# Attention's output kept with features on partitions: one product on GpSimd in place of turns on TensorE

## The chip, the cores and the metric

The kernel runs on one core of a Trainium2 chip. Its five engines work side by side, each through its own list of instructions in order: TensorE (PE) multiplies matrices into PSUM, VectorE (DVE) and ScalarE (ACT) work elementwise and can read PSUM, GpSimd (POOL) works elementwise on SBUF alone, and SyncE (SP) does nothing here but issue transfers. ScalarE issues some transfers too. The metric is the device time of one launch in microseconds; lower is better.

## The reference

One input x of 2048 rows and 640 features goes through two branches, and a gate mixes them per row:

```python
g = _sigmoid((x * gate_w).sum(-1, keepdims=True))
a = _A_ref(x, A_wq, A_wk, A_wv, A_wo, A_beta)
b = _B_ref(x, B_w1, B_w3, B_w2)
return g * a + (1 - g) * b
```

Branch b is a gated FFN of width 1728: `(silu(x @ w1) * (x @ w3)) @ w2`. Branch a is attention with 32 heads of 20 features over 4 segments of 512 rows, plus a memory that is carried from segment to segment:

```python
logits = jnp.einsum("bhqd,bhkd->bhqk", qs, ks) * scale + mask
p = _softmax(logits, axis=-1)
a_dot = jnp.einsum("bhqk,bhkd->bhqd", p, vs)
pq = phi(qs)
num = jnp.einsum("bhld,bhde->bhle", pq, M)
den = jnp.einsum("bhld,bhd->bhl", pq, z)[..., None] + 1e-6
a_mem = num / den
o = g * a_mem + (1.0 - g) * a_dot
...
M = M + jnp.einsum("bhld,bhle->bhde", pk, vs)
z = z + jnp.einsum("bhld->bhd", pk)
```

Here `phi(t)` is t + 1 above zero and exp(t) below, g is a sigmoid of one number per head, and the mask adds -1e9 where the key's row lies before the query's, so a query sees itself and later keys. The heads' outputs, side by side, are multiplied by `wo`.

## The kernel before

**Precision.** Dense products run as three passes over operands split into a rounded part and a rest (`split`, L91: ScalarE copies the rounded part, GpSimd or VectorE subtracts). Queries and keys are split in three bfloat16 parts (`split3`).

**Dense work.** The segments c = 0 to 3 are handled in two pairs, A = (0, 1) and B = (2, 3). For each pair the program projects v, k and q, builds the memory (`memory_turn`, `memory_write`), and runs the FFN in five groups of hidden blocks (`ffn_up`, `ffn_down`) and the output projection (`oproj`). Each of these is a generator that yields an estimate in ns after every piece of work.

**Attention.** `attention` (L598) walks one head at a time over 4 x 32 heads, in ten steps per head: the scores and their row maxima (`s_unit`), then, three heads later, the transposed scores with the maxima taken off through three extra rows of the query operand (`st_unit`), exp on ScalarE, zeroing of the triangle on GpSimd (L551), and for every four heads the product with v (`pv_quad`, L556). v carries a column of ones, so that the product also holds the softmax sums. In `pv_quad` the four heads stand at partitions 0, 32, 64 and 96: 20 features, the sum, and 11 unused rows. ScalarE copies the result to `oq` (L565).

**The step of the output.** One head later `o_quad` (L570) turns `oq` with four TensorE transposes (L581) into PSUM, so that rows of x lie on partitions. VectorE takes reciprocals of the sums (L584), multiplies by 1 - g (L585) and scales (L589, L592). Where there is a memory (c > 0), GpSimd adds the result to memory's part (L593), which has been loaded into the ring `oring` (L578). `oproj` needs features on partitions again: `turn` transposes the ring's blocks (L646 to L652), and each is split from PSUM (L92, L93).

**Memory's read.** `memory_read` (L258) makes, for four row blocks and two halves of the heads, the products of phi(q) with the memory (L272), then four VectorE instructions (L277 to L280): add 1e-6, reciprocal, times g, scale. The result `gm` goes to DRAM (`gd`) by SyncE and comes back by L578.

**What sets the order.** The main loop at the end lays dense pieces between attention's steps: a segment's dense estimates are spread evenly over its steps as a credit. `braid(a, b, n)` puts one piece of b after every n pieces of a and the rest of b behind a; `weave(a, b, n)` puts all of b behind piece n of a. TensorE's list stands as the source has it. The lists of the other four engines, SyncE's included, are put in order by a planner that simulates the program.

**Transfers by counted steps.** `store_later` puts a store off by four steps. Weights go through `w_load` (a transfer into one of `NRAW` = 2 raw buffers), `w_split` (four steps later, into one of `NW` = 6 tiles) and `w_get`, which forces both where they have not happened. `load_pair` (L472) loads queries and keys of two heads (`qst`, `kst`) into one of three places; `max_rows` (L522) sends the maxima's rows into `qst` (L526).

Of the kernel before, what the change touches and what calls it, by code (L numbers as in the profile page):

```python
# [26 lines left out]
NST, NW, NRAW, NHT, NVG, ND = 3, 6, 2, 6, 2, 3  # L27
KR = 6 * DH
LAG_T, LAG_P, NP, AGE = 3, 4, 4, 4
# [5 lines left out]
def gated_mix(ctx: ExitStack, tc: tile.TileContext, xT, wqk, wv, w13, w2, w2h, wo, beta, out):  # L35
# [10 lines left out]
    gd = [dp.tile([P, 4, D], F32, name=f"gd{c}") for c in range(NSEG)]  # L46
# [3 lines left out]
    mask = cp.tile([P, L], F32, name="mask")  # L50
# [3 lines left out]
    cH = cp.tile([P, H], F32, name="cH")  # L54
    nsT = [cp.tile([P, 32], BF, name=f"ns{i}") for i in range(2)]
    oring = cp.tile([P, 4, 960], F32, name="oring")
# [4 lines left out]
    def constants():  # L61
# [10 lines left out]
        nc.scalar.activation(gH, gH, AF.Exp, scale=-1.0)  # L72
        nc.vector.tensor_scalar(gH, gH, 1.0, None, op0=ALU.add)
        nc.vector.reciprocal(gH, gH)
        nc.vector.tensor_scalar(cH, gH, -1.0, 1.0, op0=ALU.mult, op1=ALU.add)
# [40 lines left out]
    raws, clock = [], dict(step=0, oldest=0, next=0)  # L116
# [141 lines left out]
    def memory_read(c):  # L258
        pq = big.pop(("q", c))[:, :KB * L].rearrange("p (b n) -> p b n", b=KB)
        for qb in range(4):  # L260
            gm = ht_tile([P, D], F32, f"gm{c}_{qb}")
            for hf in range(2):
                ps = dense_bank(f"nd{c}_{qb}_{hf}")
                nd = ps[:, :16 * VE].rearrange("p (h e) -> p h e", e=VE)
                todo = []
                for b in range(KB):
                    a0, a1 = HEADS[b]
                    u0, u1 = max(a0, 16 * hf), min(a1, 16 * hf + 15)
                    if u0 <= u1:
                        todo.append((b, a0, u0, u1))  # L270
                for n, (b, a0, u0, u1) in enumerate(todo):
                    nc.tensor.matmul(nd[:, u0 - 16 * hf:u1 - 16 * hf + 1, :],  # L272
                                     pq[:, b, qb * P:(qb + 1) * P],
                                     Ms[c - 1, b][:, u0 - a0:u1 - a0 + 1, :],
                                     start=n == 0, stop=n == len(todo) - 1, skip_group_check=True)
                r = sp.tile([P, 16], F32, tag="r16", name="nd_r")
                nc.vector.tensor_scalar(r, nd[:, :, DH], 1e-6, None, op0=ALU.add)  # L277
                nc.vector.reciprocal(r, r)
                nc.vector.tensor_mul(r, r, gH[:, 16 * hf:16 * hf + 16])
                nc.vector.tensor_mul(  # L280
                    gm[:, 320 * hf:320 * hf + 320].rearrange("p (h e) -> p h e", e=DH),
                    nd[:, :, :DH], r.unsqueeze(2).broadcast_to([P, 16, DH]))
                yield 700
            store_later(gd[c][:, qb, :], gm, ("g", c, qb))

    def v_blocks(c, iv):
# [7 lines left out]
        for lb in range(4):  # L294
# [5 lines left out]
            for hf in range(2):  # L300
# [77 lines left out]
    def job_read(c):  # L378
        return 5.6, memory_read(c)

    def job_v(cs):
        iv = [w_add(wv[i], D + 2) for i in range(KB)]
        return [(17.8, v_blocks(c, iv)) for c in cs]
# [86 lines left out]
    oall, heads = {}, {}  # L470

# [50 lines left out]
    def max_rows(j):  # L522
# [3 lines left out]
        nc.sync.dma_start(heads[j]["pair"][KR:KR + 3].rearrange("a h (b n) -> a (h b) n", n=P), mr[:24])  # L526
# [29 lines left out]
    def pv_quad(j):  # L556
# [9 lines left out]
        bank["ot"] = ot  # L566
# [3 lines left out]
    def o_quad(j):  # L570
        c, h = heads[j]["c"], heads[j]["h"]
        g, hl = h // 16, h % 16
        if hl == 0:
            at = 320 * ((2 * c + g) % 3)
            oall[c, g] = oring[:, :, at:at + 320]
            if c:
                assert ("g", c, 3) in stored
                nc.sync.dma_start(oall[c, g], gd[c][:, :, 320 * g:320 * g + 320])  # L578
        pt = pp.tile([P, L], F32, tag="o", name=f"oc{j}", bufs=1)
        for qb in range(4):  # L580
            nc.tensor.transpose(pt[:, qb * P:(qb + 1) * P], bank["ot"][:, qb * P:(qb + 1) * P], ident)  # L581
        o = pt.rearrange("p (b h e) -> p b h e", b=4, e=32)
        rc = sp.tile([P, 4, 4], F32, tag="rc", name="rc")
        nc.vector.reciprocal(rc, o[:, :, :, DH])  # L584
        nc.vector.tensor_mul(rc, rc, cH[:, h:h + 4].unsqueeze(1).broadcast_to([P, 4, 4]))  # L585
        rb = rc.unsqueeze(3).broadcast_to([P, 4, 4, DH])
        dst = oall[c, g][:, :, DH * hl:DH * hl + 4 * DH].rearrange("p b (h e) -> p b h e", e=DH)
        if c == 0:
# [273 lines left out]
```

## Time and profile before

| | us |
|---|---|
| median of 3 runs | 1186.91 |
| lowest, highest | 1186.42, 1190.69 |
| the profiled execution's own time | 1187.66 |
| its span | 1185.9 |

The profile shows one execution: busy time of each engine, windows by stage, groups of equal instructions with their mean length and the idle time before them with what ended it, waits, the chain of work that ended last, and the timeline. L12 is line 12 of the kernel before. PEld is TensorE's loading of weights, beside its matmuls. SPq and ACTq are the queues from which SyncE and ScalarE issue transfers. The granted TensorE clock is 1.0 over the whole span.

### The profile page before, as it was taken

The numbers are of one execution on the slowest core, as the hardware profiler recorded it, in microseconds if no ns is written. First come the engines' busy times: TensorE is split into PE (matmuls) and PEld (weight loads), VectorE is DVE, ScalarE is ACT, GpSimd is POOL, SyncE is SP. The second block draws the span as 40 slices with busy tenths as digits, with TensorE's granted clock in tenths as the row PEclk, the third lists the DMA queues.
The fourth block names the chain that finished last, engine by engine and source line by source line (L and its number), as shares of the span: only waits on it lengthen the run. The fifth ranks groups of instructions, "written<-read, shape, count | busy, mean of one in ns | idle before, by whom it ended". The sixth has DMA issues, their size and how long they took to land.

```text
span 1185.9 us, 20067 instructions
## 1 busy us (share of the span) xinstructions
PE 1157.3 (98%) x7093; PEld 884.9 (75%) x7093; DVE 674.0 (57%) x2186; ACT 493.3 (42%) x955; POOL 470.7 (40%) x591
## 2 busy tenths in 40 slices
PE   8989999999999999999999999999999999999998
PEld 5977766767767887877967667677767776776997
DVE  6034566456755553566245787756676676663434
ACT  6255434444244233153355554435543344334131
POOL 6065434154144234245065543334343344335232
PEclk9999999999999999999999999999999999999999
DMA  8474632232233143315257674263323243321012
GB/s 287 149 221 167 231 95 69 73 100 69 57 90 90 57 140 85 101 51 170 99 184 241 191 240 141 79 179 84 97 68 96 73 119 79 85 68 46 23 56 89
DMA packets 99460, 137.58 MB, mean 116 GB/s; under 512 B 9120, under 2 KB 69024, under 8 KB 99360
## 3 DMA queue, kind: packets, MB, share of 16 engines
q1 hardware_dynamic: 83616, 117.69, 33.4%
q10 hardware_dynamic: 15744, 18.62, 4.5%
q8 instruction: 56, 0.92, 0.3%
q14 instruction: 44, 0.36, 0.1%
HBM read 89.75 MB, written 46.14 MB: 115 GB/s over the span
## 4 chain that ended last, share of the span: by engine, by line
PE 79%; DVE 7%; issue 6%; DMA 3%; ACT 2%; POOL 2%; SPq 0%; DVEq 0%; ACTq 0%; POOLq 0%
PE g L206 16%; PE u L206 15%; PE f L458 13%; PE o L562 6%; PE s L499 6%; PE op L665 5%; PE q L206 4%; PE t L537 4%; PE v L306 3%; PE k L206 2%; POOL W L93 2%; PE nd L272 1%; PE pm L361 1%; DVE junk L506 1%; PE oc L581 1%
## 5 line engine op out<-in xcount | busy, mean ns | idle before, releaser
L506 DVE CUSTOM_DVE_ANT_0 junk<-s,mask 128x128 bf16<-128x128 f32 (+3 forms) x512 | 249.7, 488 | 204.2 <-PE s L499 195.0
L545 ACT ACTIVATE P<-t 128x384 f32<-128x384 f32 (+1 forms) x384 | 201.8, 527 | 331.7 <-PE t L542 118.6
L93 POOL TENSOR_TENSOR W<-wr,W 128x640 fp32r<-128x640 f32 (+1 forms) x126 | 196.9, 1567 | 166.9 <-ACT W L92 152.6
L551 POOL TENSOR_SCALAR_AFFINE_SELECT P<-P 128x256 f32<-128x256 f32 x256 | 105.0, 411 | 351.0 <-ACT P L545 338.4
L206 PE MATMUL g<-X,W 128*128 128x512 f32 x840 | 242.2, 423 | 0.0
L206 PE MATMUL u<-X,W 128*128 128x512 f32 x780 | 227.1, 426 | 0.0
L458 PE MATMUL f<-W,ht 128*128 128x320 f32 x1312 | 224.6, 321 | 1.9 <-DVE acc L463 1.9
L458 PEld LDWEIGHTS f<-W,ht 128*128 128x128 f32 x1312 | 199.2, 189 | 8.3 <-DVE acc L463 2.6
L206 PEld LDWEIGHTS g<-X,W 128*128 128x128 f32 x840 | 152.4, 190 | 25.9 <-issue 1.9
L206 PEld LDWEIGHTS u<-X,W 128*128 128x128 f32 x780 | 141.7, 191 | 22.1 <-issue 1.2
L499 PE MATMUL s<-kst,qst 120*128 120x128 bf16 (+3 forms) x512 | 135.4, 305 | 4.2 <-DVE m L506 2.3
L92 ACT CAST W<-wr 128x640 fp32r<-128x640 f32 (+1 forms) x133 | 95.4, 724 | 61.8 <-DMA wr<-in_w_dram 22.1
L463 DVE SCALAR_TENSOR_TENSOR acc<-f,cgate,acc 128x320 f32<-128x320 f32 x128 | 70.1, 550 | 59.6 <-PE f L458 59.0
L93 POOL TENSOR_TENSOR ht<-ft,ht 128x512 fp32r<-128x512 f32 x52 | 67.4, 1296 | 81.4 <-ACT ht L92 80.9
L537 PE MATMUL t<-qst,kst 123*128 123x512 bf16 (+1 forms) x256 | 93.1, 364 | 1.0 <-ACT P L545 1.0
L665 PE MATMUL op<-W,oT 128*128 128x320 f32 x480 | 87.7, 326 | 1.3 <-POOL W L93 0.6
L499 PEld LDWEIGHTS <-qst 120*128 120x128 bf16 x512 | 44.4, 99 | 56.2 <-issue 46.9
L206 PE MATMUL q<-X,W 128*128 128x512 f32 x300 | 81.6, 415 | 3.0 <-POOL X L93 1.1
L206 PE MATMUL k<-X,W 128*128 128x512 f32 x300 | 80.3, 412 | 2.0 <-DVE ks_t L239 2.0
L306 PE MATMUL v<-W,X 128*128 128x320 f32 (+1 forms) x480 | 76.6, 317 | 1.8 <-ACT W L92 0.8
L665 PEld LDWEIGHTS op<-W,oT 128*128 128x128 f32 x480 | 73.2, 190 | 3.9 <-POOL W L93 1.5
L562 PE MATMUL o<-P,vg 128*32 128x512 f32 (+3 forms) x1024 | 75.5, 436 | 0.0
(106 smaller groups left out, 1271.5 us busy)
## 6 DMA issues: line engine op xcount, KB each, us to landing
wr<-in_w_dram SPq DMA_DIRECT2D x80, 320.0 KB
qst<-qd SPq DMA_DIRECT2D x64, 240.0 KB
kst<-kd SPq DMA_DIRECT2D x64, 240.0 KB
qd<-qs ACTq DMA_DIRECT2D x20, 384.0 KB
kd<-ks SPq DMA_DIRECT2D x20, 384.0 KB
wr<-in_wqk_dram SPq DMA_DIRECT2D x21, 320.0 KB
wr<-in_wo_dram SPq DMA_DIRECT2D x20, 320.0 KB
vg<-vd SPq DMA_DIRECT2D x16, 336.0 KB
```

What stands on the lines that cost most here:

```text
L92: pin(nc.scalar.copy(dst[:, 0], src))
L93: (lo or nc.gpsimd.tensor_sub)(dst[:, 1], src, dst[:, 0].bitcast(F32))
L206: nc.tensor.matmul(ps, w[:, a, kb * P:(kb + 1) * P], x[:, b, kb, :], start=n == 0, stop=n == 14)
L306: nc.tensor.matmul(ps[:, :n1 - n0], x[:, a, kb, lb * P:(lb + 1) * P], wvt[kb][:, b, n0:n1], start=n == 0, stop=n == 14)
L458: nc.tensor.matmul(ps[:, :320], a, b, start=n == 0, stop=n == len(ms) - 1)
L499: nc.tensor.matmul(ps[:, o:o + n], q[:KR, qb * P:(qb + 1) * P], k[:KR, :n], start=qb != 1, stop=qb != 0, skip_group_check=True)
L506: nc.vector.tensor_tensor_reduce(out=junk[:, :n], in0=ps[:, o:o + n], in1=mask[:, L - n:], scale=1.0, scalar=-3.0e38, op0=ALU.add, op1=ALU ...
L537: nc.tensor.matmul(ps[:, :n], k[:KR + 3, t * P:(t + 1) * P], q[:KR + 3, t * P:], start=True, stop=True)
L545: last["exp"] = nc.scalar.activation(P32[:, o:o + n], src, AF.Exp, scale=SCALE)
L551: nc.gpsimd.affine_select(d, d, pattern=[[0, 2], [1, P]], base=0, channel_multiplier=-1, compare_op=ALU.is_ge, fill=0.0)
L562: nc.tensor.matmul(ps[32 * i:32 * i + 32, kb * P:], u["v"][:, kb], u["P32"][:, o:o + n], start=kb == 0, stop=kb == 3, skip_group_check=True)
L665: nc.tensor.matmul(ps[:, :320], oT[:, qb % 2, a, kb * P:(kb + 1) * P], ws[kb][:, b, 320 * hf:320 * hf + 320], start=n == 0, stop=n == 14)
```

## The change

- `pv_quad`'s output stays with features on partitions. ScalarE sends the four rows of sums from `oq` to a small tile of 128 x 16; VectorE takes reciprocals and multiplies by 1 - g there (`o_scale`, 10 steps later); SyncE stores that to DRAM (13) and reads it back spread over each head's 32 partitions (`o_sums`, 17); GpSimd multiplies `oq` by it (8 more); SyncE moves each head's 20 rows into blocks of 128 features, `oall` (`o_quad`, 12 after the read); where a block is full and there is a memory, SyncE reads memory's part and GpSimd adds it (`o_add`, 6 and 6 more). Steps are attention's, counted by `after` and `tick`.
- `memory_read` turns `gm` with TensorE transposes (L298 of the changed kernel, `turn`), ScalarE copies them out of PSUM, and ScalarE's queue stores them, features on rows.
- `oproj` has no transposes: `part` splits the `oall` blocks directly. It starts later, within the next FFN block.
- SyncE's list stands in the source's order. For that, the maxima's row transfer is put off by four steps, pair loads go by the same counter, and `w_load` waits `LEAD` = 3 steps after a split. `NRAW` is 3. The last use of the weights of v and of the output projection frees them one by one.
- The mask is bfloat16. The attention loop is one head shorter.

```diff
-NST, NW, NRAW, NHT, NVG, ND = 3, 6, 2, 6, 2, 3
+NST, NW, NRAW, NHT, NVG, ND = 3, 6, 3, 6, 2, 3
-LAG_T, LAG_P, NP, AGE = 3, 4, 4, 4
+LAG_T, LAG_P, NP, AGE, LEAD, NO = 3, 4, 4, 4, 3, 7
...
-    gd = [dp.tile([P, 4, D], F32, name=f"gd{c}") for c in range(NSEG)]
+    rd = [dp.tile([4, L], F32, name=f"rd{i}") for i in range(2)]
+    gd = [dp.tile([D, L], F32, name=f"gd{c}") for c in range(NSEG)]
...
-    mask = cp.tile([P, L], F32, name="mask")
+    mask = cp.tile([P, L], BF, name="mask")
...
+        clock["free"] = clock["step"] + (LEAD if last else 0)
...
-        if len(raws) < NRAW and clock["next"] < min(len(items), clock["oldest"] + NW):
+        if len(raws) < NRAW and clock["step"] >= clock["free"] and clock["next"] < min(len(items), clock["oldest"] + NW):
             w_load()
...
+        def turn(q0, k0):
+            ks = range(k0, min(k0 + 2, KB))
+            pt = dense_bank(f"gt{c}_{q0}_{k0}")
+            for k in ks:
+                for qb in (q0, q0 + 1):
+                    at = (2 * (k - k0) + qb - q0) * P
+                    nc.tensor.transpose(pt[:, at:at + P], gms[qb][:, k * P:(k + 1) * P], ident)
+            n = 2 * P * len(ks)
+            g = f_tile(f"gT{c}_{q0}_{k0}")
+            nc.scalar.copy(g[:, :n], pt[:, :n])
+            store_later(gd[c][k0 * P:(k0 + len(ks)) * P, q0 * P:(q0 + 2) * P].rearrange("(k p) n -> p k n", p=P),
+                        g[:, :n].rearrange("p (k n) -> p k n", k=len(ks)), ("g", c, q0, k0 // 2), nc.scalar)
+
+        for q0 in (0, 2):
+            for n in range(4):
+                read(q0 + n // 2, n % 2)
                 yield 700
-            store_later(gd[c][:, qb, :], gm, ("g", c, qb))
+            yield 1
+            yield 1
+            for k0 in (0, 2, 4):
+                turn(q0, k0)
+                yield 440
...
+                    if last and (lb, hf) == (3, 1):
+                        clock["oldest"] = iv[kb] + 1
...
+    def after(n, f, *a):
+        soon.append([n, f, a])
+
+    def tick():
+        for e in list(soon):
+            e[0] -= 1
+            if e[0] <= 0:
+                soon.remove(e)
+                e[1](*e[2])
...
-        nc.sync.dma_start(heads[j]["pair"][KR:KR + 3].rearrange("a h (b n) -> a (h b) n", n=P), mr[:24])
+        after(4, nc.sync.dma_start, heads[j]["pair"][KR:KR + 3].rearrange("a h (b n) -> a (h b) n", n=P), mr[:24])
...
-        bank["ot"] = ot
+        r = sp.tile([P, 16], F32, tag="rs", name=f"rs{j}", bufs=1)
+        nc.scalar.dma_start(r, ot[DH::32].rearrange("i (a n) -> i a n", n=16))
+        d = rd[j // 4 % 2]
+        after(10, o_scale, j, r)
+        after(13, nc.sync.dma_start, d.rearrange("i (a n) -> (i a) n", n=16), r)
+        after(17, o_sums, j, ot, d)
...
+    def o_scale(j, r):
+        h = heads[j]["h"]
+        here(nc.vector.reciprocal(r, r))
+        nc.vector.tensor_scalar(r, r, cQ[:, h // 4:h // 4 + 1], None, op0=ALU.mult)
+
+    def o_sums(j, ot, d):
+
+        sums = sp.tile([P, L], F32, tag="sums", name=f"sums{j}", bufs=1)
+        nc.sync.dma_start(sums, d.unsqueeze(1).broadcast_to([4, 32, L]))
+        after(8, lambda: here(nc.gpsimd.tensor_mul(ot, ot, sums)))
+        after(12, o_quad, j, ot)
+
+    def o_quad(j, ot):
+
         c, h = heads[j]["c"], heads[j]["h"]
...
+        for i in range(4):
+            r0 = DH * (h + i)
+            while r0 < DH * (h + i + 1):
+                b = r0 // P
+                r1 = min(DH * (h + i + 1), (b + 1) * P)
+                if (c, b) not in oall:
+                    oall[c, b] = cp.tile([P, L], F32, tag="oall", name=f"oall{c}_{b}", bufs=NO)
+                p0 = 32 * i + r0 - DH * (h + i)
+                nc.sync.dma_start(oall[c, b][r0 - b * P:r1 - b * P], ot[p0:p0 + r1 - r0])
+                if r1 == (b + 1) * P:
+                    after(6, o_add, c, b)
+                r0 = r1
+
+    def o_add(c, b):
+
+        if c:
+            assert {("g", c, 0, b // 2), ("g", c, 2, b // 2)} <= stored
+            g = sp.tile([P, L], F32, tag="sums", name=f"gq{c}_{b}", bufs=1)
+            nc.sync.dma_start(g, gd[c][b * P:(b + 1) * P])
+            after(6, lambda: here(nc.gpsimd.tensor_add(oall[c, b], oall[c, b], g)))
+        after(6, turned.append, (c, b))
...
-                        load_pair(t + 1)
+                        after(1, load_pair, t + 1)
...
+        def part(qb):
             if qb == 0:
...
+                assert (c, KB - 1) in turned
+                oT.append(big_tile(f"oT{c}", FR)[:, :4 * D].rearrange("p (q a n) -> p q a n", q=2, a=2))
+            for b in range(KB):
+                split(oT[0][:, qb % 2, :, b * P:(b + 1) * P], oall[c, b][:, qb * P:(qb + 1) * P],
+                      lo=nc.vector.tensor_sub, pin=here)
...
-    seg = [braid(d, o1, 4), o2] + jobs_group(A, 3)
+    seg = [d, weave(u, o1, 15), o2] + [job_up(A, j) for j in GROUPS[3][1:]] + [job_down(A, 3)]
...
-    with _tile.TileContext(nc, schedule_with_timeline_sim=True) as tc, tc.manual_schedule(engines={_mybir.EngineType.PE}):
+    with _tile.TileContext(nc, schedule_with_timeline_sim=True) as tc, tc.manual_schedule(engines={_mybir.EngineType.PE, _mybir.EngineType.SP}):
```

More of the change, by code (lines that the diff above doesn't have):

```diff
@@ L114, in w_add @@
         return len(items) - 1
-    raws, clock = [], dict(step=0, oldest=0, next=0)
+    raws, clock = [], dict(step=0, oldest=0, next=0, free=0)
     def w_load():
@@ new lines, in o_sums @@
+    def o_sums(j, ot, d):
[4 more added lines that the diff above has]
+    def o_quad(j, ot):
+        c, h = heads[j]["c"], heads[j]["h"]
+        for i in range(4):
+            r0 = DH * (h + i)
[9 more added lines that the diff above has]
+                r0 = r1
@@ L605, in attention @@
                     pv_quad(jp - 3)
-                elif kind == "o" and 0 <= jo < NJ and jo % 4 == 3:
-                    o_quad(jo - 3)
                 elif kind == "t":
@@ L674, in rest @@
                     yield 450
-        return turn(0), rest()
+                if qb < 2:
+                    part(qb + 2)
+        return first(), rest()
     def store(c, qb=None):
@@ L810, in gated_mix @@
             w_step()
+            tick()
 _INS = ["xT", "wqk", "wv", "w13", "w2", "w2h", "wo", "beta"]
```

150 lines of the change are left out of this document (58 added, 92 removed).

## The prediction

> **What bounds the kernel now.** I read the page first, then the windows by stage, the chain, and the instruction groups. On the page, the line of engines and the chain's shares say which engine sets the end:
>
> ```profile
> span 1185.9 us, 20067 instructions
> ...
> PE 1157.3 (98%) x7093; PEld 884.9 (75%) x7093; DVE 674.0 (57%) x2186; ACT 493.3 (42%) x955; POOL 470.7 (40%) x591
> ...
> PE 79%; DVE 7%; issue 6%; DMA 3%; ACT 2%; POOL 2%; SPq 0%; DVEq 0%; ACTq 0%; POOLq 0%
> ```
>
> TensorE is busy 98% of the span, and no other engine passes 57%. The windows (columns: start:end, length, then busy us of PE, PEld, DVE, ACT, POOL, then clock and DMA) show that this holds in each stage:
>
> ```profile
> 0.00:62.00 62.00, 57.05 (x316) 48.95 (x317) 19.91 (x30) 27.11 (x56) 23.67 (x32) 1.00 0.63 209
> 62.00:160.00 98.00, 93.13 (x477) 73.75 (x476) 48.54 (x125) 46.23 (x83) 50.22 (x62) 1.00 0.59 194
> ...
> 640.00:730.00 90.00, 85.83 (x551) 59.23 (x550) 70.26 (x252) 45.29 (x86) 38.85 (x55) 1.00 0.66 209
> ...
> 985.00:1101.00 116.00, 116.00 (x718) 82.23 (x717) 65.56 (x224) 46.73 (x88) 46.96 (x62) 1.00 0.23 65
> 1101.00:1186.00 85.00, 80.15 (x482) 74.41 (x480) 35.43 (x65) 17.33 (x33) 22.59 (x16) 1.00 0.18 59
> ```
>
> From 985 to 1101 us TensorE has no idle time at all. The idle 28.6 us (1185.9 - 1157.3) lie in the two head windows (5.0 and 4.9), in the stage where DVE is 78% busy (4.2 of 640 to 730), in the last window (4.9), and thinly elsewhere. A busy record of a matmul overlaps its neighbour, so I take prices from distances between starts. The chain, in order of time, has the densest stretch:
>
> ```profile
> 166.65 5.57 DMA kst<-kd
> ...
> 750.13 2.29 PE o L562 x32
> 773.64 2.29 PE o L562 x32
> ...
> 1149.12 10.41 PE g L206 x45
> ```
>
> 45 matmuls in 10.41 us are 0.231 us each, back to back. Loading their weights takes 0.190 us:
>
> ```profile
> L206 PEld LDWEIGHTS g<-X,W 128*128 128x128 f32 x840 | 152.4, 190 | 25.9 <-issue 1.9
> ```
>
> [...]
>
> So the forecast is a balance of TensorE time: work taken from it or given to it, and waits of it removed or made.
>
> **The change part by part.** *Transposes.* The rows of what goes:
>
> ```profile
> L581 PE MATMUL oc<-ident,oq 128*128 128x128 f32 x128 | 19.3, 273 | 0.3 <-ACT oq L565 0.3
> L646 PE MATMUL ot<-ident,oring 128*128 128x128 f32 x64 | 15.2, 278 | 0.8 <-DVE oT L93 0.8
> L649 PE MATMUL ot<-ident,oring 128*128 128x128 f32 x12 | 3.3, 273 | 0.0
> L651 PE MATMUL ot<-ident,oring 128*64 128x128 f32 x8 | 1.7, 298 | 0.0
> L652 PE MATMUL ot<-ident,oring 128*64 128x128 f32 x8 | 1.7, 298 | 0.0
> ```
>
> Those are 128 + 64 + 12 + 16 = 220. The new transposes of memory's part are 3 reads x 20 = 60. Net 160 fewer. The price of one, from the timeline (start, length, what, count):
>
> ```profile
> 266.63 0.60 PE L581 MATMUL oc<-ident,oq 128*128 128x128 f32 x4
> 266.96 0.53 PEld L206 LDWEIGHTS g<-X,W 128*128 128x128 f32 x3
> 266.99 0.95 PE L206 MATMUL g<-X,W 128*128 128x512 f32 x3
> ```
>
> Four start at 266.63 and the next matmul at 266.99: 0.36 us, 0.09 each. The record's length (0.60 / 4 = 0.15) is the upper end. 160 x 0.09 = **-14.4 us**, at most -24. I take the distance because the stream behind it is full.
>
> *Memory's read.* Each of 8 reads per chunk still ends in four DVE instructions, and now transposes of its result stand on TensorE soon after. One read's chain on DVE, and one that came late:
>
> ```profile
> 698.76 0.17 DVE L277 TENSOR_SCALAR nd_r<-nd 128x16 f32<-128x16 f32 x1
> 698.96 0.25 DVE L278 RECIPROCAL nd_r<-nd_r 128x16 f32<-128x16 f32 x1
> 699.25 0.18 DVE L279 TENSOR_TENSOR nd_r<-nd_r,gH 128x16 f32<-128x16 f32 x1
> 699.46 0.49 DVE L280 TENSOR_TENSOR gm<-nd,nd_r 128x320 f32<-128x320 f32 x1
> 699.87 0.17 DVE L277 TENSOR_SCALAR nd_r<-nd 128x16 f32<-128x16 f32 x1
> ```
>
> ```profile
> 691.03 0.85 PE L272 MATMUL nd<-Ms,pq 128*128 128x147 f32 x6
> ...
> 691.67 0.94 PE L206 MATMUL q<-X,W 128*128 128x512 f32 x3
> ...
> 694.71 0.49 DVE L280 TENSOR_TENSOR gm<-nd,nd_r 128x320 f32<-128x320 f32 x1
> ...
> 695.34 0.96 PE L272 MATMUL nd<-Ms,pq 128*128 128x84 f32 x6 [2.33 <-DVE gm L280]
> ```
>
> DVE needs 1.11 us per read (698.76 to 699.87), TensorE 0.64 (691.03 to 691.67); with the row maxima between, a result came 4.2 us after its matmuls began (691.03 to 695.20). The memory read has 18 pieces now instead of 8, but is still laid between 10 pieces (chunks 1 and 3) or 5 (chunk 2) of other work; the rest follows with attention alone between. So the second half of the reads of chunks 1 and 3 and both halves of chunk 2, four places, run four reads and then the transposes. Per place DVE has 4 x 1.11 = 4.4 us and 1 to 3 us of maxima and FFN or query work; TensorE has 4 x 0.64 = 2.6 us and 1 to 4 us of other matmuls. I estimate waits of 1.9, 2.1, 1.0 and 2.5 us, 7.5 in sum; the 2.3 us above is replaced by them: **+5**. Bounds: 0 (the scheduler finds room) and four whole latencies, 4 x 4.2 = 17.
>
> *Waits that go or come.* TensorE's waits of the kind that the edit touches, from the view of waits (total, times, longest), the third from SyncE's own:
>
> ```profile
> PE pm L361 <- ACT pkn L348: 3.3, 2, 3.1
> PE k L206 <- DVE ks_t L239: 2.0, 2, 1.2
> ...
> SPq L526 <- DVE m L506: 138.4, 30, 10.5
> ```
>
> A third raw weight buffer, weights released one at a time by the last of v and of the output projection, and the free time counted after a split all bring weights earlier; counted in the source's steps, nine weights were asked for before their load had been issued, and now none. The 3.3 us stood behind weight casts on ScalarE. I take 3.3 and 2.0 as gone by half, and 1 us of the output projection's: **-3.5**. Coming: five weights are wanted while still raw, and the first pair of heads is loaded when attention starts, not in the head: **+1**; bounds 0 and 5.57, the one landing in the chain.
>
> *Other engines, at nothing.* GpSimd gets 32 products and 15 sums of 128x512, loses 24 sums; DVE loses the reciprocals and products of the quads, and its 48 splits become 80 small ones:
>
> ```profile
> L93 POOL TENSOR_TENSOR ht<-ft,ht 128x512 fp32r<-128x512 f32 x52 | 67.4, 1296 | 81.4 <-ACT ht L92 80.9
> L593 POOL TENSOR_TENSOR oring<-oring,os 128x320 f32<-128x320 f32 x24 | 21.0, 873 | 10.7 <-DVE os L592 8.0 <-DVE ns L518 2.2 <-DVE ns L519 0.5
> ```
>
> 47 x 1.296 - 21.0 = +40 us, so GpSimd is at 511 us, 43%. What hides it is its idle 60%; the product waits on a transfer, and behind it in line are the triangle masks that the next P.V needs. They have 40 steps until then. ScalarE gets 18 copies out of PSUM, 32 more casts and 50 issues of transfers, all while 58% idle. If that cover failed, each late quad would hold TensorE by up to its 1.3 us, 32 x 1.3 = 42 us.
>
> *SyncE.* It issues 144 moves of rows, 32 + 32 sums and 15 reads of memory's part more, 18 of the old transfers less, and all in the source's order. A quad takes 40 steps: 773.64 - 750.13 = 23.5 us, 0.59 us a step in that quick stage. Pair loads are issued about 11 steps before their first use (6.5 us), row transfers of the maxima 10 steps away from them, the quad's transfers in between. 5.57 us, the worst landing shown, fits; cost nothing, up to the rival below.
>
> **The sum.** -14.4 + 5 - 3.5 + 1 = -11.9. The profiled execution's span is 1185.9 and its time 1187.7; 1187.7 - 11.9 = 1175.8. It lies 0.8 above the median of the runs, 1186.9, so 1175 to 1176; I say **1176 us**. With the bounds: 24 saved and no new wait gives about 1160; 14.4 saved against 17 + 5.6 gives 1193 to 1196.
>
> **The rivals.** *The read turns eat the gain.* The waits at the four places come near their bound (12 to 15 us) because DVE is 78% busy in the window of chunk 2. For: the late result above. Against: the first transposes need only half the result. Time: 1187.7 - 14.4 + 13 - 2 = 1184, within 0.5%.
>
> *SyncE's order makes pairs late (slower).* In the old order SyncE stood 4.6 us on average in front of a maxima transfer (138.4 / 30) and nothing on TensorE suffered. In the fixed order a quad goes through four or five transfers in a row, each waiting for the one before it to land, and everything behind stands. Where SyncE is held more than 0.9 us (6.5 - 5.57) when a pair load is due, TensorE waits for that pair. In the two quick stages are some 36 pairs; 1 us each gives 1176 + 36 = 1212, and 5 us in all against the 12 decides nothing. It needs more than 12 us of such waits, a third of a us per pair, to end slower than before. Against: there are four steps, 2.4 us, between the store of the sums and their reading, and eight before the product. [...]
>
> *More than I count.* Longer prices for the transposes (0.12) and all touched waits gone: 160 x 0.12 = 19, and 6 of waits, against 5: 1187.7 - 20 = 1168.
>
> *TensorE is not the bound.* Then the saved time becomes other waits, 1187. The full window 985 to 1101 speaks against it, and so does the gapless stretch of 45 matmuls.
>
> **How the numbers follow.** Forecast (1169 to 1181) 0.50; more than counted (1160 to 1169) 0.10; eaten by the turns (1181 to 1193) 0.18; TensorE not the bound (1187) 0.04; SyncE or GpSimd late (over 1193) 0.18. The range 1163 to 1193 leaves out most of the last and the outer part of the second. A measurement of this kernel tells 0.5%, 6 us, from no change: faster 0.60, same 0.22, slower 0.18.
>
> **What the changed profile would show.** Right: TensorE with 160 fewer records and busy time about 14 lower in proportion of starts; waits of the new transposes or of their neighbours on DVE's gm of 5 to 10 us; GpSimd near 511 us; hardly any TensorE wait on a pair load; fewer idle us in the head. Wrong: TensorE waiting for qst or kst again and again; ScalarE's or DVE's idle time ended by the sums' transfer; waits on gm above 12 us; or a span that fell by more than 20 us.

## The result and the profile after

| | before | after |
|---|---|---|
| median, us | 1188.80 (4 runs, 1186.42 to 1192.13) | 1235.82 (4 runs, 1235.24 to 1239.68) |
| ratio, 95% interval | 1 | 1.040 [1.0364, 1.0437] |
| profiled execution: time, span | 1187.66, 1185.9 | 1239.68, 1237.7 |
| mean granted TensorE clock | 1.000 | 0.981 |

The change makes the kernel 47 us slower; 1176 us with a range of 1163 to 1193 had been forecast. In both tables below, spans are compared with the span of before, 1185.9.

From the page of the changed kernel: busy time by engine, TensorE's clock in 40 slices, the chain's shares, and the group of weight casts.

```profile
PE 1164.1 (94%) x6933; PEld 883.7 (71%) x6933; DVE 692.8 (56%) x2188; ACT 500.5 (40%) x1006; POOL 508.6 (41%) x614
...
PEclk9999999999999999988999989999999999999999
...
PE 22%; DMA 7%; issue 2%; DVE 2%; SPq 1%; ACT 1%; POOL 1%; POOLq 0%; ACTq 0%; DVEq 0%
...
L96 ACT CAST W<-wr 128x640 fp32r<-128x640 f32 (+1 forms) x133 | 96.0, 727 | 211.2 <-DMA wr<-in_w_dram 129.4
```

TensorE has the forecast 160 records fewer (6933 against 7093), GpSimd the forecast busy time (508.6), and yet TensorE is busy longer in a longer span. The last row is the one to read: ScalarE's casts of weights (L96) are as long as before, but 211.2 us of ScalarE's idle time now stand in front of them, 129.4 of it ended by the landing of a weight. The same group before:

```profile
L92 ACT CAST W<-wr 128x640 fp32r<-128x640 f32 (+1 forms) x133 | 95.4, 724 | 61.8 <-DMA wr<-in_w_dram 22.1
```

What TensorE itself waits for (total, times, longest), after:

```profile
PE t L580 <- ACT P L588: 16.0, 11, 2.5
PE f L489 <- DVE acc L494: 8.8, 5, 3.4
PE v L335 <- ACT W L96: 6.7, 2, 4.7
PE s L542 <- DMA kst<-kd: 6.5, 5, 2.6
PE gt L298 <- DVE gm L288: 4.4, 5, 1.8
```

The largest wait is for the exp of attention (`P`). Exp takes its turn on ScalarE, behind casts that stand waiting for a weight: in all 13 of TensorE's waits for `P` (L580 and L583, 17.5 us) a cast that had stood 3.0 to 6.4 us for its weight's transfer came shortly before. One of them, ScalarE and then TensorE:

```profile
1045.92 0.72 ACT L96 CAST W<-wr 128x640 fp32r<-128x640 f32 x1 [5.57 <-DMA wr<-in_w_dram]
```

```profile
1048.23 0.48 PE L580 MATMUL t<-qst,kst 123*128 123x384 bf16 x1 [2.54 <-ACT P L588]
```

The pair loads (`kst`), which the prediction's slower rival had named, are fourth.

SyncE's waits of the changed kernel say where the weights' delay comes from:

```profile
SPq L512 <- DVE m L549: 217.3, 33, 11.5
SPq L512 <- DVE rs L621: 67.1, 25, 11.8
...
SPq L512 <- DVE acc L494: 49.5, 4, 21.3
```

These three are waits in front of a maxima's row or a store of the sums (L512 is a helper's line), and everything behind them in the fixed list waits too. In sum SyncE does not stand longer than before: over all rows of that view it waits 1005 us in the kernel before and 881 in the changed one. What differs is what stands behind each wait. One spot shows the whole path. SyncE after (start, length, what, count):

```profile
528.72 1.38 SPq L126 DMA_DIRECT2D wr<-in_wv_dram  x3
550.89 0.75 SPq L512 DMA_DIRECT2D qst<-mr  x1
551.70 3.10 SPq L641 DMA_DIRECT2D oall<-oq  x4
...
560.63 1.71 SPq L126 DMA_DIRECT2D wr<-in_wv_dram  x2
```

ScalarE and TensorE after, in the same stretch:

```profile
536.84 0.73 ACT L96 CAST W<-wr 128x642 fp32r<-128x642 f32 x1 [2.90 <-DMA wr<-in_wv_dram]
537.48 2.69 ACT L96 CAST X<-xr 128x512 fp32r<-128x512 f32 x5
...
568.46 0.73 ACT L96 CAST W<-wr 128x642 fp32r<-128x642 f32 x1 [2.56 <-DMA wr<-in_wv_dram]
```

```profile
548.62 1.70 PE L489 MATMUL f<-W,ht 128*128 128x320 f32 x5 [3.36 <-DVE acc L494]
...
569.24 0.63 PE L335 MATMUL v<-W,X 128*128 128x320 f32 x1 [4.73 <-ACT W L96]
```

SyncE before, at the same work:

```profile
513.75 4.60 SPq L122 DMA_DIRECT2D wr<-in_wv_dram  x2
...
530.75 0.72 SPq L526 DMA_DIRECT2D qst<-mr  x1
535.90 2.31 SPq L122 DMA_DIRECT2D wr<-in_wv_dram  x2
```

Before, the planner sent two of v's five weights at 513.75, ahead of the maxima's row. After, three go at 528.72; ScalarE stands 2.90 us for one, the five casts of X come behind it, VectorE's work comes late behind them, and TensorE waits 3.36 for `acc`. (VectorE is also slow there: its last two subtractions of X take 2.0 us each, from 544.13 on, while GpSimd works on two weights; the quickest in this trace take 0.68. The runs do not part late from slow.) VectorE's lateness holds SyncE at the maxima's row until 550.89, so v's last two weights leave only at 560.63, behind that row, the four moves and a pair load. TensorE waits 4.73 for one of them: a delay of a weight has come back as a delay of the next weight.

The clock adds to it. Windows of the changed kernel (start:end, length, busy of the five engines, clock, DMA share, GB/s):

```profile
545.00:555.00 10.00, 6.64 (x31) 5.80 (x31) 8.60 (x21) 0.60 (x1) 2.56 (x2) 0.66 0.06 15
565.00:575.00 10.00, 4.76 (x23) 1.78 (x27) 0.97 (x2) 2.46 (x4) 4.54 (x4) 0.57 0.60 199
722.00:732.00 10.00, 7.67 (x38) 6.18 (x39) 7.43 (x28) 2.95 (x5) 4.35 (x4) 0.83 0.65 186
```

Around those waits the granted clock is 0.57 to 0.83, where before it was 1.0 over the whole span. Windows cut more finely show it at half:

```profile
545.95:552.75 6.80, 4.13 (x14) 3.64 (x15) 6.04 (x17) 0.60 (x1) 1.61 (x1) 0.50 0.00 1
566.45:576.60 10.15, 6.36 (x37) 2.65 (x38) 0.18 (x1) 2.26 (x4) 4.68 (x5) 0.50 0.45 150
```

When the clock first fell in this stretch, at 545.95, TensorE had waited 2.84 and 1.86 us and then 0.7 us of the 3.36; the second time it fell 1.9 us into the wait of 4.73.

A balance of the span can be made from three numbers of each profile: TensorE's idle gaps above 0.15 us, summed over its records; the time lost to the clock, at most (1 - clock) x span; and the rest, which is work.

| kernel | span | gaps | clock | rest against before |
|---|---|---|---|---|
| before | 1185.9 | 23.0 | 1.000 | 0 |
| after | 1237.7 | 68.7 | 0.981 | 51.8 - 45.7 - 23.5 = -17.4 |

The clock's term is an upper bound, and so is the gain in work. Counted only while TensorE is busy, the clock cost 19.9 us in this trace, and the rest is -13.8. Either way the work got shorter by about what was forecast, and waits and the clock took four to five times as much back.

### The profile page after: what moved, and what is told of

The parts are those of the page before. It is cut to its first block, busy times and chain, and to the rows that moved or that the text cites. A ratio compares the mean times of both kernels' runs of the same rounds, so it can differ in the third digit from the quotient of the medians.

```text
span 1237.7 us, 20264 instructions
## 1 busy us (share of the span) xinstructions
PE 1164.1 (94%) x6933; PEld 883.7 (71%) x6933; DVE 692.8 (56%) x2188; ACT 500.5 (40%) x1006; POOL 508.6 (41%) x614
## 5 line engine op out<-in xcount | busy, mean ns | idle before, releaser
L96 ACT CAST W<-wr 128x640 fp32r<-128x640 f32 (+1 forms) x133 | 96.0, 727 | 211.2 <-DMA wr<-in_w_dram 129.4
L580 PE MATMUL t<-qst,kst 123*128 123x512 bf16 (+1 forms) x256 | 94.1, 367 | 18.5 <-ACT P L588 16.0
L211 PE MATMUL q<-X,W 128*128 128x512 f32 x300 | 85.3, 431 | 3.7 <-POOL X L97 1.9
L711 PE MATMUL op<-W,oT 128*128 128x320 f32 x480 | 84.5, 328 | 3.1 <-ACT W L96 1.9
L335 PE MATMUL v<-W,X 128*128 128x320 f32 (+1 forms) x480 | 79.2, 323 | 8.2 <-ACT W L96 6.7
L335 PEld LDWEIGHTS v<-W,X 128*128 128x128 f32 x480 | 74.5, 194 | 10.0 <-ACT W L96 7.2
L627 POOL TENSOR_TENSOR oq<-oq,sums 128x512 f32<-128x512 f32 x32 | 41.7, 1304 | 91.4 <-DMA sums<-rd 43.9
```

The source lines that it names most:

```text
L96: pin(nc.scalar.copy(dst[:, 0], src))
L211: nc.tensor.matmul(ps, w[:, a, kb * P:(kb + 1) * P], x[:, b, kb, :], start=n == 0, stop=n == 14)
L580: nc.tensor.matmul(ps[:, :n], k[:KR + 3, t * P:(t + 1) * P], q[:KR + 3, t * P:], start=True, stop=True)
L711: nc.tensor.matmul(ps[:, :320], oT[0][:, qb % 2, a, kb * P:(kb + 1) * P], ws[kb][:, b, 320 * hf:320 * hf + 320], start=n == 0, stop=n == 14)
```

## The experiments

Theory A: weights are cast too soon behind their loads. Theory B: SyncE stands before the maxima's rows and holds everything behind them. Theory C: the turns of the memory's read make TensorE late. Theory D: the output's chain of transfers fills SyncE. Theory E: SyncE's fixed order costs by itself.

**SyncE planned again.** Only SyncE leaves the list of engines that keep the source's order:

```diff
-tc.manual_schedule(engines={_mybir.EngineType.PE, _mybir.EngineType.SP})
+tc.manual_schedule(engines={_mybir.EngineType.PE})
```

> The changed kernel with one edit: SyncE's list is put in order by the planner again, as before; everything else of the change stays. Theory A (late weights: in the source's order a weight's load leaves 4.9 us before its cast instead of 15.0, ScalarE stands at the casts 211 us instead of 62, exp and the matmuls behind it are late, and the granted clock falls to 0.98): 1180 to 1200 us, idle before the W casts back under 100 us, clock 1.000. Theory B (SyncE stands in front of the maxima's rows, 20 us at 530 to 551 us, and all that is behind it is late): also most of the 48 us back, 1185 to 1205. Theory C (the transposes of memory's read wait on VectorE): no change, 1230 to 1240. Theory D (the new chain of five transfers holds GpSimd, 45 us on gq and 44 us on sums): 1225 to 1245, GpSimd's waits unchanged.

1247.5 us, 1.0503 [1.0473, 1.0533]: slower still, and above every expected range. The casts' idle time fell to 40.9 us, but TensorE now waits for pairs:

```profile
PE s L542 <- DMA kst<-kd: 33.6, 17, 4.0
PE t L580 <- DMA qst<-mr: 6.7, 5, 3.1
```

So neither of the two orders serves all transfers: the fixed one makes weights late, the planned one pairs.

**Casts later; maxima later; reads spread.** One edit each:

```diff
-LAG_T, LAG_P, NP, AGE, LEAD, NO = 3, 4, 4, 4, 3, 7
+LAG_T, LAG_P, NP, AGE, LEAD, NO = 3, 4, 4, 10, 3, 7
```

> The changed kernel with one number changed: a weight is cast 10 steps after its load instead of 4 (AGE); SyncE stays in the source's order. A: ScalarE's idle time before the W casts falls from 211 us to under 100, time 1195 to 1215. B: the maxima's rows still hold SyncE, 1225 to 1240. C: no change, 1230 to 1240. D: no change.

1223.1 us, 1.0302 [1.0269, 1.0335]; idle before casts 113.1. Both lie short of what A expected; A is a part, 13 us.

```diff
-        after(4, nc.sync.dma_start, heads[j]["pair"]...
+        after(9, nc.sync.dma_start, heads[j]["pair"]...
```

> The changed kernel with one number changed: the maxima's rows are sent 9 steps after the last scores instead of 4; SyncE stays in the source's order. B: SyncE's waits at that line fall from some 480 us to under 250, time 1195 to 1215. A: casts still wait on their transfers, 1225 to 1240. C and D: no change.

1291.5 us, 1.0857 [1.0809, 1.0906]: TensorE waits 43.9 us for the rows themselves. They have no five steps to spare, so this run could not test B; its remedy is worse than the fault.

```diff
-    seg += [braid(g[0], job_read(1), 2)] + g[1:] ...
+    seg += [braid(g[0], job_read(1), 1)] + g[1:] ...
...
-    seg += q[:2] + [q[2], braid(q[3], job_read(2), 1)]
+    seg += q[:2] + [braid((q[2][0] + q[3][0], (y for _, g in q[2:] for y in g)), job_read(2), 1)]
...
-    seg = [braid(up[0], job_read(3), 2), ...
+    seg = [braid(up[0], job_read(3), 1), ...
```

> The changed kernel with memory's reads spread over other work: one piece of a read after every piece of the FFN block (chunks 1 and 3; before it was one after two, with the rest behind), and for chunk 2 one after every piece of two query blocks instead of one. C: TensorE's waits on gm (some 10 us) fall to under 4 us, time 1220 to 1230. A, B and D: 1230 to 1240.

1227.4 us, 1.0343 [1.0302, 1.0384]. TensorE's waits on `gm` fell from 6.3 to 2.3 us, as C expected, and the time by 8 us; the interval still overlaps that of the changed kernel (from 1.0364), so C is a small part at most.

**The other half of the change alone.** The kernel before with the weights' edits, the bfloat16 mask and the counted steps, with SyncE's order fixed and with SyncE planned; `os` goes through an f tile for space.

```diff
-NST, NW, NRAW, NHT, NVG, ND = 3, 6, 2, 6, 2, 3
+NST, NW, NRAW, NHT, NVG, ND = 3, 6, 3, 6, 2, 3
...
+        clock["free"] = clock["step"] + (LEAD if last else 0)
...
-        nc.sync.dma_start(heads[j]["pair"]...
+        after(4, nc.sync.dma_start, heads[j]["pair"]...
...
-                        load_pair(t + 1)
+                        after(1, load_pair, t + 1)
...
-tc.manual_schedule(engines={_mybir.EngineType.PE})
+tc.manual_schedule(engines={_mybir.EngineType.PE, _mybir.EngineType.SP})
```

> The other half of the change alone: the kernel before with three raw weight buffers, weights released one by one, the bfloat16 mask, and SyncE's list in the source's order with the counted maxima rows and pair loads; output and memory's part as before (the scaled quad goes through one of the f tiles in place of a tile of its own, for space). Theory D (the output's new chain of transfers is what fills SyncE's list and holds it): without the chain the order costs nothing; 1178 to 1192 us, TensorE's idle time near 20 us. Rival E (SyncE's fixed order with counted steps costs by itself, because each transfer stands behind the one before it): 1205 us or more, with waits for weight casts or pair loads as in the changed kernel.

> As the run beside it, but SyncE's list planned as in the kernel before: what the weights' edits alone bring. Both theories: 1180 to 1190 us. Together with the changed kernel (1236), the planned one with the new output (1248) and the run beside it this fills a square of output path and SyncE's order. D expects the column of the old output to lie near 1187 under both orders; E expects only this corner to do so.

Fixed: 1207.3 us, 1.0148 [1.012, 1.0175]. Planned: 1184.3 us, 0.9963 [0.9948, 0.9977]. E is true as well: fixing the order costs 23 us with nothing of the new output in the kernel. D in its strict form, that the order costs nothing without the chain, is refuted. Beside E the new output adds 29 us (1207.3 to 1235.8) under the fixed order and 63 under the planner's; how much of that is the chain, the next runs ask. The planned one is the fastest of all kernels run here.

What the fixed order does is seen at the output projection of segment 0. SyncE and then TensorE with the fixed order:

```profile
394.31 0.73 SPq L484 DMA_DIRECT2D qst<-mr  x1
404.71 0.33 SPq L495 DMA_DIRECT2D qst<-qd  x1
405.10 0.43 SPq L495 DMA_DIRECT2D kst<-kd  x1
405.58 0.58 SPq L499 DMA_DIRECT2D vg<-vd  x1
406.26 1.05 SPq L122 DMA_DIRECT2D wr<-in_wo_dram  x2
```

```profile
407.29 0.68 PE L682 MATMUL op<-W,oT 128*128 128x320 f32 x3
412.82 0.64 PE L682 MATMUL op<-W,oT 128*128 128x320 f32 x1 [4.84 <-ACT W L92]
```

SyncE stands from 395.0 to 404.7 in front of a pair load; its waits at that line (L495) are for TensorE's `t` and `s`, which read the place to be filled. The last two weights of the projection, which need no such place, stand behind it, and TensorE waits 4.84 us. With SyncE planned, the last weight of the projection goes ahead of that pair:

```profile
376.67 0.36 SPq L122 DMA_DIRECT2D wr<-in_wo_dram  x1
...
399.46 0.32 SPq L495 DMA_DIRECT2D qst<-qd  x1
399.84 0.43 SPq L495 DMA_DIRECT2D kst<-kd  x1
```

**Two parts of the chain left out.** One move of 128 rows per quad in place of four or five of 20 or fewer (the rows go to wrong places):

```diff
-                nc.sync.dma_start(oall[c, b][r0 - b * P:r1 - b * P], ot[p0:p0 + r1 - r0])
...
+        nc.sync.dma_start(oall[c, b], ot)
```

> The changed kernel with one move of 128 rows per quad into a block in place of four or five of 20 rows or fewer (the rows go to the wrong place): 112 issues of SyncE fewer, 82 us at the 0.73 us that one takes in the changed kernel's trace. If the moves' issue time on SyncE is the greater part of the chain's price: 1195 to 1210 us, and ScalarE's idle time before weight casts falls from 211 us to below 120. If it is the waiting of the chain's steps for each other (sums stored, read back, multiplied): 1225 us or more.

The sums' way left out (no division; `oq` times blocks of the identity):

```diff
-        nc.scalar.dma_start(r, ot[DH::32].rearrange("i (a n) -> i a n", n=16))
...
-        after(10, o_scale, j, r)
-        after(13, nc.sync.dma_start, d.rearrange("i (a n) -> (i a) n", n=16), r)
-        after(17, o_sums, j, ot, d)
+        after(17, o_sums, j, ot)
...
-        nc.sync.dma_start(sums, d.unsqueeze(1).broadcast_to([4, 32, L]))
-        after(8, lambda: here(nc.gpsimd.tensor_mul(ot, ot, sums)))
+        after(8, lambda: here(nc.gpsimd.tensor_mul(o3, o3, ident.unsqueeze(1).broadcast_to([P, 4, P]))))
```

> The changed kernel without the sums' way through DRAM (no division: GpSimd multiplies by the identity's blocks instead; the four transfers and two VectorE instructions per quad are left out), the moves as they are. If the round trip holds SyncE and GpSimd and so makes the rest late: 1195 to 1215 us, with GpSimd's 44 us before the product gone. If the moves alone fill SyncE: 1225 us or more.

1223.1 us, 1.0287 [1.0254, 1.0319], and 1216.2 us, 1.0224 [1.0195, 1.0253]: 13 and 20 us. Both lie between the two ranges that were expected: neither the moves' issue time nor the sums' way is the whole price, and the few transfers that wait for each other cost more than the many moves. 112 issues fewer, by the expectation 82 us of SyncE's time, were worth 13, so most of that issue time did not count.

**The maxima's rows from ScalarE's queue,** on the old output and on the changed kernel:

```diff
-        after(4, nc.sync.dma_start, heads[j]["pair"]...
+        after(4, nc.scalar.dma_start, heads[j]["pair"]...
```

> The run with the old output and SyncE's order fixed (1207), with the maxima's row transfers issued by ScalarE's queue in place of SyncE's. If SyncE's standing in front of these rows (225 us in that run) is what makes weight loads late behind it: 1185 to 1195 us, and ScalarE's idle time before weight casts falls from 106 us towards 30. If other waits on SyncE's list do it (on TensorE's units for pair loads, 205 us): still 1200 us or more. If ScalarE's own holding costs as much: over 1210.

> The same edit on the changed kernel (1236). If the hold at the maxima's rows is common to both: 1205 to 1220 us. If the output's transfers hold SyncE by themselves and take its place: 1225 us or more.

1208.4 us, 1.0163 [1.0132, 1.0194], and 1236.5 us, 1.0399 [1.0364, 1.0433]: no change in either. The casts' idle time fell (105.7 to 70.5 us with the old output, 211.2 to 178.9 in the changed kernel), but TensorE's waits for the output projection's weights hardly did (8.8 to 7.8 us with the old output). SyncE's waits with the old output, with the rows on SyncE and then without:

```profile
SPq L484 <- DVE m L521: 225.3, 32, 11.0
SPq L495 <- PE t L557: 132.1, 33, 11.0
...
SPq L495 <- PE s L514: 72.5, 23, 6.7
```

```profile
SPq L495 <- PE t L557: 380.8, 33, 26.2
SPq L495 <- PE s L514: 240.3, 22, 14.4
```

The 225 us in front of the maxima are gone, and the waits in front of pair loads went from 205 to 621. In the changed kernel the store of the sums took the place (67.1 to 279.1 us). Whichever transfer is next in the list holds it until the attention's pace lets it go. So the maxima's rows are not a cause of their own. (ScalarE now waits for those rows itself: 25.4 us of its idle time before an exp end with VectorE's maxima in the run with the old output. What that took back is not parted.)

**Both parts of the chain out, and with later casts and spread reads as well** (edits as above):

> The changed kernel with one move per quad and without the sums' way through DRAM, both cuts in one (rows in the wrong place, no division). The cuts alone gave 13 and 20 us. If they free the same SyncE time, 1210 to 1216; if they add, 1200 to 1206; by the prediction's transposes (-14) on top of the run with the old output (1207) a chain that cost nothing would give 1193.

> As the run beside it, and weight casts 10 steps behind their loads in place of 4 (13 us alone), reads of the memory spread over twice as many pieces (8 us alone). If the loss is late casts plus the turns of the read plus the chain, each as measured alone: 1180 to 1192 us. If over 1200, something else of the change still holds, and the sum of the single effects was not a sum.

1212.6 us, 1.0204 [1.0163, 1.0245], and 1200.4 us, 1.011 [1.006, 1.016]. 13 and 20 together gave 23, not 33: they free the same time. And with nearly the whole chain gone, the changed order still costs.

**Three repairs.** The constants of `cQ` loaded and computed behind the head:

```diff
     stores(True)
+    constants_late()
     att = attention()
```

> The changed kernel with the second set of gate constants (cQ) loaded and computed behind the head in place of within it. In the changed kernel's trace ScalarE stands 6.3 us in the head before the exp of cQ, TensorE waits 2.0 us at the first v soon after, and the first P.V quad comes 6.8 us late. If that is the head's whole loss: 1228 to 1231 us and the first quad within 1 us of the kernel before. If the new waits later swallow it: 1234 us or more.

> The changed kernel with three repairs that leave all its work in place: constants behind the head (7 us expected), weight casts 10 steps behind their loads (13 us alone), reads of the memory spread over twice as many pieces (8 us alone). If they add: 1208 us. If they free the same time: 1215 to 1223.

> The run without the chain and with later casts and spread reads (1200), with the constants behind the head. If the head's 7 us were the last thing that no run had taken away: 1192 to 1195 us. It is the bound of what the change can give with SyncE's order fixed and its chain of transfers free.

1230.5 us, 1.034 [1.0297, 1.0384], too near the changed kernel's interval to count. Its first quad came later (190.4 us against 188.0 in the changed kernel and 181.2 before), because the first pair's load now stood behind the constants: TensorE waited 8.6 us for `kst`, where the changed kernel waited 2.6. The head's loss was moved, not removed. The three repairs together gave 1224.5 us, 1.0292 [1.0265, 1.0318]; the single differences of 13 and 8 do not add. Without the chain, 1208.2 us, 1.0147 [1.0119, 1.0176], no better than without this repair.

**Later casts with the old output** (`AGE` 10):

> The run with the old output and SyncE's order fixed (1207), with weight casts 10 steps behind their loads. If what SyncE's order costs by itself is that loads are issued just ahead of the casts (4.2 us in the middle in that run, 15.0 in the kernel before), so that ScalarE stands before them: 1188 to 1195 us, and ScalarE's idle time before weight casts under 50. If it is something else of the order: over 1202.

1203.3 us, 1.0108 [1.0081, 1.0135]. The casts' idle time fell to 61.6 us, that of the kernel before (61.8), and some 13 us of loss (1.0108) were still there. A does not explain E: the total of idle time does not tell. That it matters which weight is late fits this, but was not tried by itself.

**Weights from ScalarE's queue.** The last pair of runs takes the weight loads out of SyncE's list and leaves the order of the rest, on the old output and on the changed kernel:

```diff
-        nc.sync.dma_start(raw[:, :n], src)
+        nc.scalar.dma_start(raw[:, :n], src)
```

> The run with the old output and SyncE's order fixed (1207), with the weight loads issued by ScalarE's queue, which the planner orders, and all other transfers of SyncE as they were. If the order's price is that weight loads stand on SyncE behind pair loads and maxima rows that wait for TensorE and VectorE (taking the maxima away alone only let the pair loads wait longer, 205 to 621 us): 1183 to 1192 us, and TensorE's 8.8 us before the output projection's weights gone. If over 1202: it is not the weights' place behind those waits.

> The same edit on the changed kernel (1236). If the late weights are the greater part of its loss too: 1200 to 1212 us, with the idle time before weight casts below 90. If the output's transfers make pair loads late by themselves: 1215 us or more, with TensorE waits on kst.

1191.5 us, 1.0021 [1.001, 1.0033], and 1200.8 us, 1.0111 [1.0077, 1.0145]: 16 of the 23 us and 35 of the 47 us are back, with one line. Both lie in the expected ranges, and with the old output TensorE's waits for the output projection's weights went from 8.8 to 0.6 us. The page's rows of the changed kernel with this edit:

```profile
PE 1151.4 (96%) x6933; PEld 876.2 (73%) x6933; DVE 688.9 (58%) x2188; ACT 500.3 (42%) x1006; POOL 508.4 (42%) x614
...
L96 ACT CAST W<-wr 128x640 fp32r<-128x640 f32 (+1 forms) x133 | 94.1, 724 | 39.8 <-PE f L489 18.7
```

The idle time before the casts is now 39.8 us, and matmuls of the FFN, not transfers, end the largest part of it (18.7). What the edit saved is what stood in front of the weights' transfers: 211.2 us of idle time before the casts in the changed kernel, 39.8 with the edit. SyncE itself stands in front of the maxima's rows as long as before (217.3 us in the changed kernel):

```profile
SPq L512 <- DVE m L549: 217.7, 35, 11.9
```

So the gain is not that SyncE stands less there, but that no weight stands behind it. (The edit works in both directions: SyncE also no longer stands before a weight's buffer, 86.2 us in the run with the old output, and ScalarE's list is placed by the planner. The runs do not part these.)

What TensorE waits for that is left, in the same kernel:

```profile
PE nd L280 <- DVE gm L288: 5.6, 2, 4.1
PE s L542 <- DMA kst<-kd: 4.6, 3, 1.7
PE s L542 <- DVE m L549: 4.4, 3, 1.9
PE t L580 <- DMA qst<-mr: 4.1, 2, 2.4
PE gt L298 <- DVE gm L288: 3.5, 5, 1.1
...
PE gt L298 <- DVE qs_t L244: 1.9, 1, 1.9
PE nd L280 <- DVE nd_r L287: 1.7, 1, 1.7
```

The runs as a square (medians, us):

| | SyncE planned | order fixed | fixed, weights on ScalarE |
|---|---|---|---|
| old output | 1184.3 | 1207.3 | 1191.5 |
| new output | 1247.5 | 1235.8 | 1200.8 |

And the balance of spans continued:

| kernel | span | gaps | clock | rest against before |
|---|---|---|---|---|
| old output, planned | 1183.0 | 19.6 | 0.999 | -2.9 + 3.4 - 1.2 = -0.7 |
| old output, fixed | 1202.9 | 32.2 | 0.993 | 17.0 - 9.2 - 8.4 = -0.6 |
| old output, weights on ScalarE | 1188.9 | 23.9 | 0.996 | 3.0 - 0.9 - 4.8 = -2.7 |
| new output, weights on ScalarE | 1197.6 | 41.1 | 0.993 | 11.7 - 18.1 - 8.4 = -14.8 |
| new output, no sums | 1211.7 | 51.1 | 0.988 | 25.8 - 28.1 - 14.5 = -16.8 |
| new output, no chain | 1206.2 | 44.3 | 0.987 | 20.3 - 21.3 - 15.7 = -16.7 |

The four kernels with the new output, the changed one among them, have 15 to 17 us less work; those with the old output 1 to 3. The runs with the new output that are not in the tables give 16 to 21 by the same sum. With the clock's loss counted only while TensorE is busy, all runs with the new output lie between 13 and 18, those with the old output between 0 and 3.

## Why the prediction was wrong

*What bounds the kernel.* Right as read: TensorE was the bound, and what was taken from its list did come off its work. But the argument from its 98% left out that an engine with so little idle time can be made late by many small waits.

*Transposes, -14.4.* Right as far as the balance tells: 160 records fewer, and 13 to 18 us less work, with the clock counted while TensorE is busy.

*Memory's read, +5.* Waits of 7.5 us were expected. With the weights out of the way the waits that are kin to the read's turns and its bank (`gm` 5.6 and 3.5, `qs_t` 1.9, `nd_r` 1.7) sum to 12.7, the size of the rival "the read turns eat the gain"; `gm` alone, 9.1, lies within the 5 to 10 that were to show the forecast right. Spreading the reads gave 8 us on the changed kernel, which is not clearly outside the noise. The mechanism was right and the term too small.

*Waits that go or come, -3.5.* This step failed first. It said that the third raw buffer and the earlier release bring weights earlier, counted in the source's steps. In steps they were earlier; in time they were not. From a load's issue to its cast the median was 15.0 us before and 4.9 us after, because a load is issued only when the transfers ahead of it in the fixed list have gone. The page's 211.2 us of ScalarE's idle time stand behind that. The first pair's wait (2.6 us against an expected 1) and the head are part of this: TensorE was 6.8 us late at the first quad, not early, with ScalarE standing 6.3 us before the exp of `cQ`; what a repair of that would give is open, since the one that was run made the pair late.

*Other engines, at nothing.* Busy time as forecast (GpSimd 508.6 against 511). The products' late transfers held GpSimd (43.9 us before them), but TensorE's waits for `P` came with the weights and went with them: over all its lines that wait goes from 17.5 to 2.5 us once the weights are on ScalarE. The cover held for GpSimd. For ScalarE it did not: it is idle 60% of the span, and 129.4 us of that is standing before a weight, with the exp behind it.

*SyncE, cost nothing.* This is the step that decided. It compared a landing of 5.57 us with 6.5 us between a pair's load and its use, and asked only whether pairs come late. It did not ask what else stands in the list behind a waiting transfer. Fixing the order costs 23 us without any new transfer; the new ones add 29 more. The rival "SyncE's order makes pairs late (slower)" had the right place and the right sign, with 1212; its victim was wrong. TensorE waited 6.5 us for pairs; moving the weights' loads off the list gave 35 of the 47 us back. Its threshold ("held more than 0.9 us") was passed in front of the maxima's rows, 6.6 us on average (217.3 / 33), and only five pairs came late; why the others did not, no run shows. With the planned order, the rival's own victim appeared: 33.6 us of waits for pairs.

*"In the old order SyncE stood 4.6 us on average in front of a maxima transfer (138.4 / 30) and nothing on TensorE suffered."* True of that row (all rows of the line sum to 294 us), and the wrong inference: nothing suffered there because the planner had put the weights ahead of it. With the planner's order the median lead of a weight is 15.0 us, and 23.7 with three raw buffers (the old output, planned); with the fixed order it is 4.2 there.

*The clock.* The prediction priced every wait at its length. The changed kernel lost up to 23.5 us to the clock on top of 45.7 us of gaps.

What stays open: the two kernels with weights on ScalarE (1191.5 and 1200.8) lie 9 us apart although the new output has 12 us less work. 17 us more of gaps and up to 4 us more of the clock make the difference; the waits for `gm`, pairs and maxima's rows account for most of the gaps, but no run parts them. How much the order of the other transfers still costs was not tried.

## What to carry to other kernels

An issuing engine's list is a resource of its own kind: what counted here was not its busy time but what stood behind a transfer that waited for another engine (112 issues fewer gave 13 us, the weights' loads on another queue 35). Loads that wait for nothing but a free buffer, such as weights, should not share a list in fixed order with transfers that wait for the pace of the work, and before an order is fixed by hand one should read what the planner had put ahead of each wait. A lead counted in program steps is no lead in time while the engine that issues is being held (here a median of 15.0 us became 4.9); and where a bound engine is nearly full, look for small waits that come close together: here the clock fell with them, and added up to 23.5 us to 45.7 us of gaps.

## What was not expected of the hardware

The granted clock fell around waits of 2 to 5 us, to 0.50 for some 7 and 10 us in the two windows shown, in the first 0.7 us into a wait of 3.36 us, in the second 1.9 us into one of 4.73; over the span it was 0.981, against 1.000 before. Moving the maxima's rows to another queue changed nothing (1.0399 against 1.040): the hold went over to the next transfer in the list, with the old output to the pair loads, from 205 to 621 us. Moving the weights gave 35 us, though the casts, the loads and their sizes were the same.
